# Float64 weights to float32 in five instructions, the scale in one step with the square, the bias as a row on the output, and the output stored by the sync engine

**The chip, the cores and the metric.** One core of a Trainium2 chip. The time is the device time of one execution in microseconds (us), the median over runs. All numbers of profiles are from one profiled execution each, in us from its start, unless ns is said. PE is the tensor engine, PEld its weight loads, DVE the vector engine, ACT the scalar engine, POOL is GpSimd, SP the sync engine; SPq and ACTq are DMA instructions that SP and ACT issue.

## The reference, cut to what matters

```python
kv  = einsum('bhsd,bhse->bhde', k, v)          # (8, 8, 576, 64) each
out = einsum('bhsd,bhde->bhse', q, kv)
x   = out / sqrt(mean(out*out) + 1e-6) * g_norm # to 4608 tokens x 512
r   = maximum(x @ w_in, 0)                      # w_in 512 x 2048, float64
g   = s * (r * r) + b                           # s, b scalars
return g @ w_out                                # w_out 2048 x 512, float64
```

The weights come as float64; the kernel turns them into float32 before it multiplies with them. Since b is one number, `g @ w_out` is `(s r r) @ w_out` plus b times the column sums of w_out, the same row for every token.

## The kernel before

The tokens are worked in twelve tiles T of 384. While the products of tile T run on PE, the attention of tile T+1 is done in 16 steps between them (four pieces of 128 features: turn q, multiply by kv, root mean square, scale). In tile 0 the 32 weight blocks of 128 x 512 are converted at the same time.

```python
    KV_BUFS, AHEAD = 2, 3
    def round_w(i):                      # nine instructions
        nc.vector.tensor_scalar(m <- hi & 0xFFFFF)
        nc.vector.tensor_scalar(e <- (hi >> 20) & 0x7FF)
        nc.scalar.activation(l, lo, AF.Copy, scale=2.0**-52)
        nc.scalar.activation(one_m, m, AF.Copy, bias=1.0, scale=2.0**-20)
        nc.vector.tensor_scalar(e <- clip(e))
        nc.vector.tensor_scalar(e <- (e - 896) * 2**23)
        nc.vector.scalar_tensor_tensor(e <- (hi & sign) | e)
        nc.gpsimd.tensor_tensor(one_m <- one_m + l)
        nc.gpsimd.tensor_tensor(w_sb[i] <- one_m * e)
    ...  # (operands abbreviated)
    def mm1(T, f):
        ...  # four matmuls into h
        nc.scalar.activation(r, h, AF.Relu)
        nc.vector.tensor_mul(r2, r, r)
        nc.vector.tensor_scalar(out=gT[T, f], in0=r2, scalar1=s_col, scalar2=b_col, op0=ALU.mult, op1=ALU.add)
    def mm2(T, j):
        ...  # sixteen matmuls into o
        nc.scalar.copy(o_sb, o)
        nc.scalar.dma_start(out=out_v[...], in_=o_sb)
    ...
    for T in range(NT):
        if 1 <= T and T + 1 < NT:
            load_q(T + 1)                # six DMAs on the sync queue
        ...
        steps = attention(T + 1) if T + 1 < NT else []
        for f in range(FC):              # 16 blocks
            if T == 0:
                w_step(f + 2)            # round_w, then load a weight
            mm1(T, f)
            if steps:
                steps[f]()               # steps[0] turns q of tile T+1 on PE
        if T == 0:
            for i in range(FC + 2, 2 * FC):
                w_step(i)
            ...
        for j in range(J):
            mm2(T, j)
            ...
```

## Time and profile before

| | before |
|---|---|
| time, median of the first 3 runs | 1290.95 us |
| tile 0 ends, tile 1 begins | 264.56 us |
| tiles 1 to 10, up to the start of the last (264.56 to 1203.52) | 938.96 us |
| one plain tile | 92.26 to 92.36 us |
| PE waits after tile 0 | 25.1 us |

The second to fourth rows are starts of the first block of a tile in PE's timeline. A plain tile is one in which no k/v product stands; with one it is 97.5 to 97.8. The profile follows back from the last instruction what released what; this chain says which engine the time hung on (shares of the span):

```profile
PE 68%; DVE 26%; ACT 2%; issue 2%; DMA 1%; SPq 1%; POOLq 0%; DVEq 0%; ACTq 0%
```

A quarter of the span hung on DVE: about 170 us of the chain in tile 0 and about 167 us behind it. The two are not worth the same. Behind tile 0 PE works beside DVE almost all the time and waits for it only 25.1 us, so no more than about that can be won there; a share of the chain is not yet a gain. The other views of before stand in the prediction.

### The profile page before, as it was taken

The numbers are of one execution on the slowest core, as the hardware profiler recorded it, in microseconds if no ns is written. First come the engines' busy times: TensorE is split into PE (matmuls) and PEld (weight loads), VectorE is DVE, ScalarE is ACT, GpSimd is POOL, SyncE is SP. The second block draws the span as 40 slices with busy tenths as digits, with TensorE's granted clock in tenths as the row PEclk, the third lists the DMA queues.
The fourth block names the chain that finished last, engine by engine and source line by source line (L and its number), as shares of the span: only waits on it lengthen the run. The fifth ranks groups of instructions, "written<-read, shape, count | busy, mean of one in ns | idle before, by whom it ended". The sixth has DMA issues, their size and how long they took to land.

```text
span 1289.6 us, 10478 instructions
## 1 busy us (share of the span) xinstructions
PE 1144.8 (89%) x4272; PEld 605.1 (47%) x4272; DVE 499.7 (39%) x700; ACT 206.8 (16%) x397; POOL 89.1 (7%) x72
## 2 busy tenths in 40 slices
PE   3465644899999999999999999999999999999998
PEld 3232411355455455455455454454554554554553
DVE  0499999235035044053053053052153161251220
ACT  0122322021022021021021021020121120120110
POOL 0054456100000000000000000000000000000000
PEclk9998755899999999999999999999999999999999
DMA  9032224300441000000631000001401000000000
GB/s 235 10 93 75 93 98 144 84 9 1 108 114 24 17 9 0 17 9 1 147 74 25 24 1 9 17 0 46 103 1 33 17 1 9 16 1 17 8 1 24
DMA packets 63664, 55.20 MB, mean 43 GB/s; under 512 B 40576, under 2 KB 48768, under 8 KB 63616
## 3 DMA queue, kind: packets, MB, share of 16 engines
q1 hardware_dynamic: 57984, 45.10, 13.6%
q10 hardware_dynamic: 5632, 9.44, 1.9%
q8 instruction: 33, 0.54, 0.2%
q14 instruction: 15, 0.12, 0.0%
HBM read 45.09 MB, written 9.44 MB: 42 GB/s over the span
## 4 chain that ended last, share of the span: by engine, by line
PE 68%; DVE 26%; ACT 2%; issue 2%; DMA 1%; SPq 1%; POOLq 0%; DVEq 0%; ACTq 0%
PE o_ps L294 38%; PE h_ps L277 23%; DVE inv L255 7%; DVE gT L285 4%; PE x_ps L235 3%; DVE r L283 3%; PE ss_ps L249 3%; DVE w_e L141 2%; DVE w_e L138 2%; DVE w_e L132 2%; DVE xT L258 2%; DVE qT L230 1%; PE kv_ps L201 1%; ACT r L281 1%; DVE w_e L144 1%
## 5 line engine op out<-in xcount | busy, mean ns | idle before, releaser
L294 PE MATMUL o_ps<-w,gT 128*128 128x512 f32 x1152 | 517.6, 608 | 40.3 <-POOL w L148 40.3
L277 PE MATMUL h_ps<-xT,w 128*128 128x384 f32 x1536 | 528.7, 493 | 20.1 <-POOL w L148 20.1
L277 PEld LDWEIGHTS h_ps<-xT,w 128*128 128x128 f32 x1536 | 291.0, 193 | 207.9 <-POOL w L148 23.8
L294 PEld LDWEIGHTS o_ps<-w,gT 128*128 128x128 f32 x1152 | 220.8, 194 | 328.2 <-issue 260.6
L283 DVE TENSOR_TENSOR r<-r 128x384 f32<-128x384 f32 x192 | 106.4, 554 | 556.1 <-ACT r L281 556.1
L281 ACT ACTIVATE r<-h_ps 128x384 f32<-128x384 f32 x192 | 93.9, 489 | 377.6 <-PE h_ps L277 363.6
L255 DVE RECIPROCAL inv<-rms 128x384 f32<-128x384 f32 x48 | 122.2, 2545 | 18.5 <-ACT rms L251 18.5
L285 DVE TENSOR_SCALAR gT<-r,s_col,b_col 128x384 f32<-128x384 f32 x192 | 105.3, 548 | 7.9
L235 PE MATMUL x_ps<-qT,bd_kv 128*128 128x192 f32 x192 | 48.1, 378 | 57.8 <-DVE qT L230 57.8
L302 ACT COPY o_sb<-o_ps 128x512 f32<-128x512 f32 x36 | 21.1, 586 | 477.7 <-PE o_ps L294 477.7
L235 PEld LDWEIGHTS x_ps<-qT,bd_kv 128*128 128x128 f32 x192 | 34.3, 209 | 82.9 <-DVE qT L230 79.2
L214 DVE COPY bd_kv<-kv_ps 64x256 f32<-64x256 f32 x8 | 3.4, 422 | 153.9 <-PE kv_ps L201 153.9
L147 POOL TENSOR_TENSOR w_1m<-w_1m,w_l 128x512 f32<-128x512 f32 x32 | 43.2, 1351 | 100.4 <-ACT w_1m L137 100.4
L148 POOL TENSOR_TENSOR w<-w_1m,w_e 128x512 f32<-128x512 f32 x32 | 44.0, 1374 | 43.8 <-DVE w_e L144 42.2
L249 PE MATMUL ss_ps<-sq,ones_bd 128*128 128x384 f32 x96 | 42.2, 523 | 2.4 <-ACT sq L243 2.4
L201 PE MATMUL kv_ps<-v_sb,k_sb 64*64 64x64 f32 x1152 | 25.5, 244 | 19.8 <-DMA v_sb<-in_v_dram 19.8
L137 ACT ACTIVATE w_1m<-w_m 128x512 f32<-128x512 uint32 x32 | 20.2, 630 | 116.2 <-DVE w_m L129 113.1
L201 PEld LDWEIGHTS kv_ps<-v_sb,k_sb 64*64 64x64 f32 x1152 | 22.9, 156 | 27.8 <-issue 23.0
L243 ACT ACTIVATE sq<-x_ps 128x384 f32<-128x384 f32 x48 | 23.5, 490 | 60.5 <-PE x_ps L235 60.5
L258 DVE SCALAR_TENSOR_TENSOR xT<-x_ps,g_col,inv 128x384 f32<-128x384 f32 x48 | 29.6, 617 | 5.3 <-DVE inv L255 0.5
L141 DVE TENSOR_SCALAR w_e<-w_e 128x512 uint32<-128x512 uint32 x32 | 31.1, 973 | 1.1
L251 ACT ACTIVATE rms<-ss_ps,eps_col 128x384 f32<-128x384 f32 x48 | 27.8, 580 | 13.3 <-PE ss_ps L249 13.3
(21 smaller groups left out, 212.1 us busy)
## 6 DMA issues: line engine op xcount, KB each, us to landing
k_sb<-in_k_dram SPq DMA_DIRECT2D x32, 288.0 KB, 4.7
v_sb<-in_v_dram SPq DMA_DIRECT2D x32, 288.0 KB, 5.7
q_sb<-in_q_dram SPq DMA_DIRECT2D x72, 128.0 KB, 3.4
out_dram<-o_sb ACTq DMA_DIRECT2D x36, 256.0 KB, 2.0
w_raw<-in_moe_w_in_dram SPq DMA_DIRECT2D x16, 512.0 KB, 3.8
w_raw<-in_moe_w_out_dram SPq DMA_DIRECT2D x16, 512.0 KB, 3.1
g_col<-in_g_norm_dram ACTq DMA_DIRECT2D x2, 0.2 KB, 2.9
s_col<-in_moe_s_dram ACTq DMA_DIRECT2D x1, 0.5 KB, 5.3
```

Of the source, the lines that this page charges most:

```text
L141: nc.vector.tensor_scalar(out=e, in0=e, scalar1=896.0, scalar2=2.0**23, op0=ALU.subtract, op1=ALU.mult)
L148: nc.gpsimd.tensor_tensor(out=w_sb[i], in0=one_m, in1=e.bitcast(FP32), op=ALU.mult)
L201: nc.tensor.matmul(kv_ps[g][s][l * HB : l * HB + HB, p, :], lhsT=kt[rows, l, j, :], rhs=vt[rows, l, j, :], start=(j == 0), stop=(j == R - 1),)
L235: nc.tensor.matmul(st["x"][:, :, s, :], lhsT=bd[:, s, p, :], rhs=st["qT"][:, :, s, :], start=True, stop=True,)
L249: nc.tensor.matmul(ps, lhsT=ones_bd, rhs=st["sq"], start=True, stop=True)
L255: nc.vector.reciprocal(inv, st["rms"])
L258: nc.vector.scalar_tensor_tensor(xT[T][:, p, :], st["x"].rearrange("p j s t -> p (j s t)"), g_col, inv, ALU.mult, ALU.mult,)
L277: nc.tensor.matmul(h, lhsT=w_in(c, f), rhs=xT[T][:, c, :], start=(c == 0), stop=(c == KC - 1))
L281: nc.scalar.activation(r, h, AF.Relu)
L283: nc.vector.tensor_mul(r2, r, r)
L285: nc.vector.tensor_scalar(out=gT[T, f], in0=r2, scalar1=s_col, scalar2=b_col, op0=ALU.mult, op1=ALU.add)
L294: nc.tensor.matmul(o, lhsT=gT[T, f][:, j * P : j * P + P], rhs=w_out(f), start=(f == 0), stop=(f == FC - 1),)
```

## The change

Its intent: fewer DVE and POOL instructions for a weight, one DVE instruction fewer for each of the 192 blocks of g, and ACT relieved of evicting the output. Cut to its core (one buffer fewer for g, and an earlier load of q for tile 1, are left out):

```diff
-    KV_BUFS, AHEAD = 2, 3
+    KV_BUFS, AHEAD = 3, 4
     def round_w(i):
-        ...  # five DVE, two ACT, two POOL instructions
+            nc.scalar.activation(y, hi, AF.Copy, scale=2.0**-112)
+            nc.scalar.activation(q3, lo, AF.Copy, scale=2.0**-29)
+            nc.vector.tensor_scalar(t <- (y << 3) & 0x7FFFFFFF)
+            nc.vector.scalar_tensor_tensor(t <- (y & sign) | t)
+            nc.gpsimd.tensor_tensor(out=w_sb[i].bitcast(U32), in0=t, in1=q3, op=ALU.add)
+        ...  # for w_out: nc.gpsimd.tensor_tensor adds w_sb[i] to wsum
     def mm1(T, f):
-        nc.vector.tensor_mul(r2, r, r)
-        nc.vector.tensor_scalar(out=gT[T, f], in0=r2, scalar1=s_col, scalar2=b_col, ...)
+        nc.vector.scalar_tensor_tensor(gT[T, f], r, s_col, r, ALU.mult, ALU.mult)
+    def bias_row():
+        nc.tensor.matmul(ps, lhsT=b_sq, rhs=wsum, start=True, stop=True)
+        nc.vector.tensor_copy(out=b_row, in_=ps)
     def mm2(T, j):
-        nc.scalar.copy(o_sb, o)
-        nc.scalar.dma_start(out=out_v[...], in_=o_sb)
+        nc.vector.tensor_tensor(out=o_sb, in0=o, in1=b_row, op=ALU.add)
+        nc.sync.dma_start(out=out_v[...], in_=o_sb)
+    for i in range(AHEAD):
+        load_w(i)                        # now ahead of the fourth k/v load
     for p in range(NP):
         kv_product(0, p)
         ...
+        # three w_steps inside the last quarter of attention(0)
     for T in range(NT):
         ...
         if T == 0:
             for i in range(FC + 3, 2 * FC):
                 w_step(i)
+            bias_row()
```

More of the change, by code (lines that the diff above doesn't have):

```diff
@@ L61 @@
     actp = ctx.enter_context(tc.tile_pool(name="actp", bufs=3))
-    gp = ctx.enter_context(tc.tile_pool(name="gp", bufs=FC + 4))
+    gp = ctx.enter_context(tc.tile_pool(name="gp", bufs=FC + 3))
     outp = ctx.enter_context(tc.tile_pool(name="outp", bufs=3))
@@ L117, in load_w @@
             nc.sync.dma_start(out=dst, in_=src[f * P : f * P + P, :])
+    wsum = const.tile([P, DM], FP32, name="wsum")
     def round_w(i):
-        if not wide:
-            return
-        raw = w_raw.pop(i).rearrange("p (n two) -> p n two", two=2)
-        lo, hi = raw[:, :, 0], raw[:, :, 1]
-        e = rawp.tile([P, DM], U32, name="w_e", tag="w_e", bufs=2)
-        m = rawp.tile([P, DM], U32, name="w_m", tag="w_m", bufs=2)
-        l = rawp.tile([P, DM], FP32, name="w_l", tag="w_l", bufs=2)
@@ L128, in round_w @@
-        one_m = rawp.tile([P, DM], FP32, name="w_1m", tag="w_1m", bufs=2)
-        nc.vector.tensor_scalar(
-            out=m, in0=hi, scalar1=0xFFFFF, scalar2=None, op0=ALU.bitwise_and
-        )
-        nc.vector.tensor_scalar(
-            out=e, in0=hi, scalar1=20, scalar2=0x7FF,
-            op0=ALU.logical_shift_right, op1=ALU.bitwise_and,
-        )
-        nc.scalar.activation(l, lo, AF.Copy, scale=2.0**-52)
-        nc.scalar.activation(one_m, m, AF.Copy, bias=1.0, scale=2.0**-20)
-        nc.vector.tensor_scalar(
-            out=e, in0=e, scalar1=896.0, scalar2=1151.0, op0=ALU.max, op1=ALU.min
-        )
@@ L141, in round_w @@
-        nc.vector.tensor_scalar(
-            out=e, in0=e, scalar1=896.0, scalar2=2.0**23, op0=ALU.subtract, op1=ALU.mult
-        )
-        nc.vector.scalar_tensor_tensor(
-            e, hi, 0x80000000, e, ALU.bitwise_and, ALU.bitwise_or
-        )
-        nc.gpsimd.tensor_tensor(out=one_m, in0=one_m, in1=l, op=ALU.add)
-        nc.gpsimd.tensor_tensor(out=w_sb[i], in0=one_m, in1=e.bitcast(FP32), op=ALU.mult)
+        if wide:
+            raw = w_raw.pop(i)
+            hi = raw.bitcast(FP32).rearrange("p (n two) -> p n two", two=2)[:, :, 1]
+            lo = raw.rearrange("p (n two) -> p n two", two=2)[:, :, 0]
+            y = rawp.tile([P, DM], FP32, name="w_y", tag="w_y", bufs=2)
+            q3 = rawp.tile([P, DM], U32, name="w_q", tag="w_q", bufs=2)
+            t = rawp.tile([P, DM], U32, name="w_t", tag="w_t", bufs=2)
+            nc.scalar.activation(y, hi, AF.Copy, scale=2.0**-112)
+            nc.scalar.activation(q3, lo, AF.Copy, scale=2.0**-29)
+            yb = y.bitcast(U32)
+            nc.vector.tensor_scalar(
+                out=t, in0=yb, scalar1=3, scalar2=0x7FFFFFFF,
+                op0=ALU.logical_shift_left, op1=ALU.bitwise_and,
+            )
+            nc.vector.scalar_tensor_tensor(
+                t, yb, 0x80000000, t, ALU.bitwise_and, ALU.bitwise_or
+            )
+            nc.gpsimd.tensor_tensor(out=w_sb[i].bitcast(U32), in0=t, in1=q3, op=ALU.add)
@@ L150, in w_step @@
+        if i == FC + 1:
+            nc.gpsimd.tensor_tensor(out=wsum, in0=w_sb[FC], in1=w_sb[FC + 1], op=ALU.add)
+        elif i > FC + 1:
+            nc.gpsimd.tensor_tensor(out=wsum, in0=wsum, in1=w_sb[i], op=ALU.add)
     def w_step(i):
@@ L187 @@
     nc.scalar.dma_start(out=b_col, in_=moe_b.to_broadcast((P, 1)))
+    b_sq = const.tile([P, P], FP32, name="b_sq")
+    nc.vector.memset(b_sq, 1.0)
+    nc.vector.tensor_scalar(
+        out=b_sq, in0=b_sq, scalar1=b_col, scalar2=None, op0=ALU.mult
+    )
+    b_row = const.tile([P, DM], FP32, name="b_row")
     kv_ps = {}
@@ L281, in mm1 @@
         nc.scalar.activation(r, h, AF.Relu)
-        r2 = actp.tile([P, N], FP32, name="r2", tag="r2")
-        nc.vector.tensor_mul(r2, r, r)
         gT[T, f] = gp.tile([P, N], FP32, name="gT", tag="g")
-        nc.vector.tensor_scalar(
-            out=gT[T, f], in0=r2, scalar1=s_col, scalar2=b_col, op0=ALU.mult, op1=ALU.add
-        )
+        nc.vector.scalar_tensor_tensor(gT[T, f], r, s_col, r, ALU.mult, ALU.mult)
+    def bias_row():
+        ps = ps_o.tile([P, DM], FP32, name="b_ps", tag="o")
+        nc.tensor.matmul(ps, lhsT=b_sq, rhs=wsum, start=True, stop=True)
+        nc.vector.tensor_copy(out=b_row, in_=ps)
     out_v = out.rearrange("(bp j) n -> bp j n", j=R)
@@ L301, in mm2 @@
         o_sb = outp.tile([P, DM], FP32, name="o_sb", tag="o_sb")
-        nc.scalar.copy(o_sb, o)
+        nc.vector.tensor_tensor(out=o_sb, in0=o, in1=b_row, op=ALU.add)
         g = T // TPG
-        nc.scalar.dma_start(out=out_v[g * P : g * P + P, T % TPG * J + j, :], in_=o_sb)
+        nc.sync.dma_start(out=out_v[g * P : g * P + P, T % TPG * J + j, :], in_=o_sb)
+    for i in range(AHEAD):
+        load_w(i)
     for p in range(NP):
@@ L310 @@
             load_kv(0, p + KV_BUFS)
-    for i in range(AHEAD):
-        load_w(i)
-    for step in attention(0):
+    load_q(1)
+    steps = attention(0)
+    for n, step in enumerate(steps):
         step()
-    load_q(1)
-    for i in range(2):
-        w_step(i)
+        if n >= 12 and n < 15:
+            w_step(n - 12)
     for T in range(NT):
@@ L328 @@
             if T == 0:
-                w_step(f + 2)
+                w_step(f + 3)
             mm1(T, f)
@@ L333 @@
         if T == 0:
-            for i in range(FC + 2, 2 * FC):
+            for i in range(FC + 3, 2 * FC):
                 w_step(i)
+            bias_row()
             for p in range(KV_BUFS):
```

## The prediction

> **What bounds the kernel now.** I read the page's rows of slices first, then the wait table of the tensor engine, then the timelines of four places. The rows (40 slices of 32.2 us) show two programs in one:
>
> ```profile
> PE   3465644899999999999999999999999999999998
> DVE  0499999235035044053053053052153161251220
> POOL 0054456100000000000000000000000000000000
> ```
>
> The reader should see that PE is full from slice 8 on, and that in slices 2 to 6 DVE is full, PE half idle and POOL busy: there the float64 weights are turned into float32 while the first of twelve token tiles runs. The wait table of PE, for the part after tile 0 (264.6 us on), has one entry:
>
> ```profile
> PE x_ps L235 <- DVE qT L230: 25.1, 30, 1.2
> ```
>
> So in 1025 us of steady work PE waits 25.1 us, 30 times some 0.83 us, always for the copy of qT on DVE. Everything else there is PE's own time. In tile 0 the timeline shows why DVE is slow:
>
> ```profile
> 101.74 0.69 DVE L144 SCALAR_TENSOR_TENSOR w_e<-w_raw,w_e 128x512 uint32<-128x512 uint32 x1
> 102.57 1.45 POOL L148 TENSOR_TENSOR w<-w_1m,w_e 128x512 f32<-128x512 f32 x1 [1.15 <-DVE w_e L144]
> 102.93 1.30 DVE L285 TENSOR_SCALAR gT<-r,s_col,b_col 128x384 f32<-128x384 f32 x1
> ...
> 458.27 0.48 DVE L285 TENSOR_SCALAR gT<-r,s_col,b_col 128x384 f32<-128x384 f32 x1
> ```
>
> The same gT instruction takes 1.30 us while POOL runs (it ends 0.2 us after POOL's end at 104.02) and 0.48 us at 458 us, where POOL is silent. The two engines take turns. The stages of tile 0 come from the next lines, again of the timeline:
>
> ```profile
> 70.72 4.73 PE L277 MATMUL h_ps<-xT,w 128*128 128x384 f32 x8 [8.80 <-POOL w L148]
> ...
> 188.37 0.69 DVE L144 SCALAR_TENSOR_TENSOR w_e<-w_raw,w_e 128x512 uint32<-128x512 uint32 x1
> ...
> 192.71 0.69 DVE L144 SCALAR_TENSOR_TENSOR w_e<-w_raw,w_e 128x512 uint32<-128x512 uint32 x1
> ...
> 233.93 30.79 PE L294 MATMUL o_ps<-w,gT 128*128 128x512 f32 x66 [2.20 <-POOL w L148]
> 264.56 2.74 PE L277 MATMUL h_ps<-xT,w 128*128 128x384 f32 x8
> ```
>
> First product from 70.7; one w_out weight each 4.34 us (192.71 minus 188.37) until about 232; one third of the second product is done under that conversion, the last two thirds in 30.8 us; tile 1 starts at 264.56.
>
> [...] 1.30 against 0.48 us above, and L144 (two SBUF inputs) took 1.65 us at 111.55 us, when POOL was at work. [...] Here the square is 0.55 us and the scale 0.48 us, and one operation with two inputs should be near the square's 0.55. [...] behind 6.2 us of waiting (98.5 to 104.75 us) the eight first-product matmuls took 3.98 us, against 2.74 us in the next group.
>
> **The change part by part.**
>
> *a. Start.* Four weight loads (2.1 MB) now stand in the queue ahead of the fourth k/v pair, without which the first attention can't begin. 2048 packets of 1 KB at about 50 ns over 16 DMA engines are 6.4 us. Three conversions move into the last quarter of that attention; most fits into waits of DVE, but the third stands before the reciprocal: about +1.7 us. The wait for the first converted weight after the attention (66 to 70.7) goes, -4.4. First product at 70.7 + 6.4 + 1.7 - 4.4 = 74.4.
>
> *b. First product of tile 0, 16 weights.* Before, four weights took 24.4 us (reciprocals at 95.8 and 120.2), 6.1 each. [...] With turns taken: from the end of the second DVE operation POOL needs 1.59 us (as 102.43 to 104.02), the blocked operation ends 0.2 later, then 0.6 for the next: 2.4 us a weight, four of them 9.7 less the last POOL operation, which hides under the reciprocal, plus copy, reciprocal and scaling of the attention, about 3.6: 12 us. PE needs 12.1 to 13 us for the same four (270.9 to 283.9 in tile 1 is 13.0, with a 0.83 wait in it). I take 13 for the coupling of the two, times four, plus 2 for the cold clock: 54 us. It ends near 129.
>
> *c. Conversion of the last 13 weights.* ACT 1.3 us a weight, DVE 1.1, POOL two operations (the addition and the running column sum), together about 2.7 us as the contiguous pair of before. DVE's first operation slips in between them, the second costs its 0.55 and a 0.15 handover: 3.45 us, 45 us in all, plus 1 for two sums under b. It ends near 175. (Before: 4.34.)
>
> *d. The bias row.* Its matmul stands ahead of the whole second product and needs all weights, so no third of it is hidden any more: 2 cold matmuls 1.8 us, then 96 x 0.449 = 43.1, and 1.2 for the clock (30.79 before, against 66 x 0.449 = 29.6). Tile 1 begins at 175 + 46 = 221, against 264.6: -43.6; rounded -43.
>
> *e. gT in one operation.* DVE loses 0.45 to 0.5 us per block; two blocks stand in front of each of the late qT copies (gT before the reciprocal and after it), so the copy comes 0.9 us earlier and the 0.83 us wait goes: up to -25, I take -24.
>
> *f. The output moves to DVE and the sync queue.* Eviction 0.75 us by DVE instead of 0.59 by ACT, hidden. But sync issues in program order. Before, it held loads alone and fetched q a tile ahead. Now the load of q for tile T+1 stands behind the three stores of tile T-1, the last of which waits for the end of that tile; and PE wants this q right after the first block of tile T. The listing of the changed kernel's instructions confirms it: three stores, then six q loads, for T = 1 to 10. Sizes, from the timeline and the q tile's own view:
>
> ```profile
> 403.24 3.99 SPq L92 DMA_DIRECT2D q_sb<-in_q_dram  x6
> ...
> DMA to landing us min/median/max: 2.7/3.1/3.3
> ...
> 454.57 0.59 ACT L302 COPY o_sb<-o_ps 128x512 f32<-128x512 f32 x1 [13.15 <-PE o_ps L294]
> ...
> 455.19 0.34 ACTq L304 DMA_DIRECT2D out_dram<-o_sb  x1
> 456.63 0.14 PEld L228 LDWEIGHTS qT_ps<-ident,q_sb 128*128 128x128 f32 x1
> 456.95 0.49 PE L228 MATMUL qT_ps<-ident,q_sb 128*128 128x128 f32 x3
> ```
>
> From the end of the product (454.5): eviction to 455.3, store issued by 455.8, sixth q load issued five steps of 0.665 later at 459.1, landed 3.2 later at 462.3; PE wants it at 457.2. Stall 5.1 us, in seven tiles; in the three tiles that follow a k/v product (2.5 us of other work for PE) 2.6 us: 43.5. The clock after 5 us of idling: about +1.5 each, 0.3 after the short ones: 11.4. Together +55.
>
> Sum: 1291 - 43 - 24 + 55 = 1279 us.
>
> **The rivals.** R1: the q loads arrive in time, since q is double-buffered, and nothing is given back: 1291 - 67 = 1224. For it: q has two buffers and DMA has room. Against: the order on one queue; a buffer does not help a load that has not been issued. R2: the stalls are worse, each with a full return to the cold clock (2.1 us measured after 6.2 us of idling), the stores delaying q in the DMA engines, and no gain in e because DVE is behind after each stall: 1291 - 43 + 75 = 1323. Against: after the stall all four blocks of DVE work lie behind PE as before. R3: POOL is still the bound of tile 0, the integer addition slower than the float one (1.27 to 1.31 us unhindered)[...]: +7 to +12, 1286 to 1291. The trace has DVE getting in between two contiguous POOL operations[...].
>
> **Range and chances.** Tile 0 I trust to 9 us, e to 5, f to 12; together about 16: 1262 to 1298 for 8 in 10. Faster by 2% is under 1265, which needs a stall near 4 us or a tile 0 ten us better: 0.16. Slower by 2% is over 1317, near R2: 0.05. Within 2%: 0.79.
>
> **What would show it.** In the profile of the changed kernel: tile 1 begins near 221; POOL has 47 additions of 128x512 (32 conversions, 15 sums), and a w_out weight takes about 3.45 us; PE is idle from about 130 to 175; the wait table after tile 0 has nothing left of x_ps for qT and instead ten waits of qT_ps for a q load, up to 5 us each, and tiles 3 to 4 us longer than before (1025 us over eleven tiles, 93 each). If PE's wait for q is absent, f is wrong and R1 holds; if POOL's addition is longer than 1.4 us without a DVE operation beside it, c is wrong; if tiles after a stall show matmuls at double length for more than 3 us, R2 holds.

The sum stays 1291 - 43 - 24 + 55 = 1279 us. What stands behind its steps, from the trace and the page of before:

- *Turns of DVE and POOL* (steps b and c): L285 takes 1.30 us beside POOL and 0.48 without, L144 1.65 (at 111.55) and 0.69 (at 101.74). How the two engines come to exclude each other is not shown. The sentence cut in b counted, for a weight, three DVE operations (two of the conversion, and gT) and one of POOL.
- *DVE between two POOL operations* (c): POOL's operations at 184.86 and 186.15 us follow without a gap; DVE's L132, begun at 184.97, ends at 186.47, 0.3 us after the first of them, and L138 then begins under the second.
- *Clock*: behind 6.2 us of waiting, four x_ps matmuls took 1.65 us (at 104.75; 0.81 at 270.05) and eight of the first product 3.98 (at 106.19; 2.74 at 110.66), at a granted clock of 0.50 from 104.75 to 108.0: 2.1 us more in all. The 2 us in b and the 1.5 and 0.3 in f are estimates; beside them stand the first block of tile 0, 4.73 us against 2.74, and the block at 95.68, 2.85 us behind a wait of 2.05. Two 128 x 512 matmuls at a granted clock of 0.50 took 2.07 us (186.23), where d takes 1.8.
- *50 ns a packet* (a): the page has 57984 packets of q1 in 13.6% of 16 engines' 1289.6 us, 48 ns each on the mean.
- *R3* had a second case; the range of +7 to +12 stood for both.

## The result, and the profile after

| | before | after |
|---|---|---|
| time, median | 1290.99 us (4 runs) | 1281.97 us (4 runs, 1281.34 to 1285.44) |
| tile 1 begins | 264.56 | 219.89 |
| from there to the start of the last tile | 938.96 | 974.08 |
| plain tiles | 92.26 to 92.36 | 92.38 to 98.09 |

The ratio is 0.9934, with a 95% interval of 0.992 to 0.9948: within 2%. A ratio is the mean time of one kernel's fast runs over that of the other's in the same rounds, so it isn't quite the ratio of the medians.

So tile 0 won 44.7 us and the other tiles gave 35.1 back. The same rows of slices of the changed kernel, with the granted clock of PE as a fourth:

```profile
PE   2488059999999899899999899899999899899998
DVE  0378930330340240240241241241241141141110
POOL 0033840000000000000000000000000000000000
PEclk9999569999999899999899899999999999999999
```

The conversion ends two slices earlier (POOL has nothing from slice 6 on, counted from 0; before from slice 8), but PE, which before was half busy under it, is empty in slice 4. And behind it there are slices of 8 in the rows of PE and of its clock, which before had none there. The chain of the changed kernel names the new holder:

```profile
PE 84%; DMA 4%; SPq 4%; DVE 4%; issue 2%; POOL 2%; ACT 1%; POOLq 0%; DVEq 0%; ACTq 0%
```

DVE fell from 26% to 4% (from about 170 to 38 us in tile 0, from 167 to 8 behind it). DMA and SPq, 2% together before, are 8%. The wait table of PE from 235 us on shows which DMA:

```profile
PE qT_ps L236 <- DMA q_sb<-in_q_dram: 35.2, 23, 4.1
```

The 25.1 us of x_ps for qT are gone, and in their place stand 35.2 us of the transposes of q for the load of q; two more waits, 4.3 us, lie in the first stall, just before 235: 39.5 us in all. One of the ten stalls, at the start of tile 3, in the order of time (start, length, then the engine):

```profile
415.54 2.74 PE L285 MATMUL h_ps<-xT,w 128*128 128x384 f32 x8
415.74 0.69 DVE L312 TENSOR_TENSOR o_sb<-o_ps,b_row 128x512 f32<-128x512 f32 x1 [13.04 <-PE o_ps L304]
416.46 0.33 SPq L314 DMA_DIRECT2D out_dram<-o_sb  x1
416.84 4.02 SPq L92 DMA_DIRECT2D q_sb<-in_q_dram  x6
422.42 0.89 PE L236 MATMUL qT_ps<-ident,q_sb 128*128 128x128 f32 x2 [4.13 <-DMA q_sb<-in_q_dram]
424.31 0.47 PE L236 MATMUL qT_ps<-ident,q_sb 128*128 128x128 f32 x1 [1.01 <-DMA q_sb<-in_q_dram]
424.58 5.16 PE L285 MATMUL h_ps<-xT,w 128*128 128x384 f32 x8
```

PE begins tile 3 at 415.54. Only then can DVE evict the last output of tile 2, SP store it, and SP send, from 416.84 on, for the q that PE wants as soon as its first block is done, near 418.2. PE stands for 4.13 us, then for 1.01, and the next block of eight matmuls takes 5.16 us instead of 2.75. Tile 0, from the timeline:

```profile
143.36 1.60 POOL L150 TENSOR_TENSOR wsum<-wsum,w 128x512 f32<-128x512 f32 x1
144.92 1.44 POOL L146 TENSOR_TENSOR w<-w_t,w_q 128x512 uint32<-128x512 uint32 x1
...
175.27 2.07 PE L296 MATMUL b_ps<-wsum,b_sq 128*128 128x512 f32 x2 [45.57 <-POOL wsum L150]
177.14 42.92 PE L304 MATMUL o_ps<-w,gT 128*128 128x512 f32 x96
219.89 2.74 PE L285 MATMUL h_ps<-xT,w 128*128 128x384 f32 x8
```

POOL has two operations a weight without a gap, 3.08 us a weight (the sum before this one began at 140.28). PE waits 45.6 us for the last of them, then does the bias row and the whole second product of tile 0.

### The profile page after: what moved, and what is told of

Its sections match the earlier page's. It is cut to its first block, busy times and chain, and to the rows that moved or that the text cites. A ratio compares the mean times of both kernels' runs of the same rounds, so it can differ in the third digit from the quotient of the medians.

```text
span 1280.2 us, 10164 instructions
## 1 busy us (share of the span) xinstructions
PE 1141.2 (89%) x4274; PEld 608.5 (48%) x4274; DVE 382.3 (30%) x451; ACT 187.4 (15%) x361; POOL 69.8 (5%) x55
## 4 chain that ended last, share of the span: by engine, by line
PE 84%; DMA 4%; SPq 4%; DVE 4%; issue 2%; POOL 2%; ACT 1%; POOLq 0%; DVEq 0%; ACTq 0%
PE o_ps L304 39%; PE h_ps L285 37%; PE x_ps L243 3%; SPq L92 3%; PE ss_ps L257 3%; DMA q_sb<-in_q_dram 3%; DVE inv L263 2%; POOL w L146 1%; PE qT_ps L236 1%; DMA k_sb<-in_k_dram 1%; DMA v_sb<-in_v_dram 1%; PE kv_ps L209 1%; DVE o_sb L312 1%; POOL wsum L150 0%; DVE gT L291 0%
## 5 line engine op out<-in xcount | busy, mean ns | idle before, releaser
L285 PE MATMUL h_ps<-xT,w 128*128 128x384 f32 x1536 | 539.0, 501 | 2.7 <-DVE xT L266 2.7
L304 PE MATMUL o_ps<-w,gT 128*128 128x512 f32 x1152 | 499.5, 594 | 0.0
L285 PEld LDWEIGHTS h_ps<-xT,w 128*128 128x128 f32 x1536 | 297.1, 197 | 193.8 <-issue 21.3
L291 DVE SCALAR_TENSOR_TENSOR gT<-r,s_col 128x384 f32<-128x384 f32 x192 | 120.7, 629 | 338.6 <-ACT r L289 338.6
L312 DVE TENSOR_TENSOR o_sb<-o_ps,b_row 128x512 f32<-128x512 f32 x36 | 24.9, 691 | 442.7 <-PE o_ps L304 442.7
L236 PE MATMUL qT_ps<-ident,q_sb 128*128 128x128 f32 x144 | 31.6, 310 | 40.8 <-DMA q_sb<-in_q_dram 39.5
L236 PEld LDWEIGHTS qT_ps<-ident,q_sb 128*128 128x128 f32 x144 | 20.8, 153 | 64.1 <-issue 50.7
L146 POOL TENSOR_TENSOR w<-w_t,w_q 128x512 uint32<-128x512 uint32 x32 | 44.7, 1397 | 103.6 <-DVE w_t L143 94.0
L296 PE MATMUL b_ps<-wsum,b_sq 128*128 128x512 f32 x2 | 2.1, 1140 | 45.6 <-POOL wsum L150 45.6
L238 DVE COPY qT<-qT_ps 128x384 f32<-128x384 f32 x48 | 26.5, 551 | 40.5 <-PE qT_ps L236 40.5
L143 DVE SCALAR_TENSOR_TENSOR w_t<-w_y,w_t 128x512 uint32<-128x512 uint32 x32 | 34.4, 1075 | 1.1
L139 DVE TENSOR_SCALAR w_t<-w_y 128x512 uint32<-128x512 uint32 x32 | 30.9, 965 | 6.0 <-ACT w_y L136 6.0
L259 ACT ACTIVATE rms<-ss_ps,eps_col 128x384 f32<-128x384 f32 x48 | 27.8, 580 | 12.7 <-PE ss_ps L257 12.7
```

Of the source, the lines that this page charges most:

```text
L146: nc.gpsimd.tensor_tensor(out=w_sb[i].bitcast(U32), in0=t, in1=q3, op=ALU.add)
L236: nc.tensor.transpose(ps[:, j, :], q_in[T][:, j, 2 * p : 2 * p + 2, :], ident)
L285: nc.tensor.matmul(h, lhsT=w_in(c, f), rhs=xT[T][:, c, :], start=(c == 0), stop=(c == KC - 1))
L291: nc.vector.scalar_tensor_tensor(gT[T, f], r, s_col, r, ALU.mult, ALU.mult)
L304: nc.tensor.matmul(o, lhsT=gT[T, f][:, j * P : j * P + P], rhs=w_out(f), start=(f == 0), stop=(f == FC - 1),)
L312: nc.vector.tensor_tensor(out=o_sb, in0=o, in1=b_row, op=ALU.add)
```

## The experiments

**Theory.** Three things make up the result: a shorter tile 0; the qT wait that went with the shorter gT; and the q load, which stands on one queue behind the stores of the tile before, so that PE waits and then works at half clock for a while (granted 0.50 for 3.41 or 6.83 us at a time, experiment 4). **Rivals** are named with each run: the eviction on DVE, the traffic of stores beside loads, a wait that only moves. All ten runs ended with a correct result within the comparison's tolerance; their time is the median of four executions, and the kernel before took 1291.6 to 1291.9 us beside them. The changed kernel was not run again beside them; its 1281.97 us is from its own rounds. Three parts of the change were never taken alone: the third k/v buffer, the fourth weight in flight, and the three conversions inside the first attention.

**Experiment 1: the stores issued by ACT again.** The changed kernel with

```diff
-        nc.sync.dma_start(out=out_v[...], in_=o_sb)
+        nc.scalar.dma_start(out=out_v[...], in_=o_sb)
```

> The changed kernel with its output stores issued by ScalarE again; all else as changed. Theory (issue order: a q load stands behind the stores and comes 4 us late, and PE then works at half clock for a while): the ten waits of qT_ps for q (39.5 us) and the slower matmuls after them (about 21 us, worked out as 1060 us for the tiles 1 to 11 minus 1025 before, plus 25 of x_ps waits gone, minus 39.5) all go: 1282 - 60 = 1222 us, within 6. Rival (the rest of the change costs the time: eviction on DVE, a later gT, or DMA traffic of stores beside loads whoever issues them): little or nothing is won, 1270 to 1282 us.

Measured: 1219.76 us, ratio 0.9441 (0.9427 to 0.9455). The wait table of PE from 215 us on is empty, every plain tile takes 89.5 to 89.7 us, and the time from the start of tile 1 to that of the last is 911.33 us, 62.75 less than the 974.08 of the changed kernel. The rival falls: eviction on DVE and the late gT, which stayed, cost nothing that can be seen.

**Experiment 2: stores on the sync queue, q ahead of them.** The changed kernel with

```diff
-        if 1 <= T and T + 1 < NT:
-            load_q(T + 1)
...
+        if T + 2 < NT:
+            load_q(T + 2)
         for j in range(J):
             mm2(T, j)
```

> The changed kernel with its stores still on the sync queue, but the q load of tile T+2 issued ahead of the three stores of tile T instead of after them. Theory (only the order on the one queue matters): as good as giving the stores back to ScalarE, 1222 us within 6, no wait of PE for q. Rival (one queue for loads and stores is too little: the stores delay the loads in the engines, or sync has no time to issue both): PE still waits for q or k/v, 1245 us or more.

Measured: 1218.54 us, ratio 0.9435 (0.9421 to 0.9449), no different from experiment 1, and no wait of PE for q. So neither the number of queues nor the traffic matters here, only what stands in front of the q load in the order of issue.

**Experiment 3: the kernel before with the stores on the sync queue,** nothing else:

```diff
-        nc.scalar.dma_start(out=out_v[...], in_=o_sb)
+        nc.sync.dma_start(out=out_v[...], in_=o_sb)
```

> The kernel before with nothing changed but the stores, issued by the sync engine. Theory: it pays the ten waits (39.5 us) and the half clock after them (about 21 us), while its own x_ps waits stay as they are: 1291 + 60 = 1351 us, within 10. Rival (in the changed kernel the waits came from its lighter DVE or its other buffers, not from the store): 1291 to 1300 us.

Measured: 1353.9 us, ratio 1.0482 (1.0467 to 1.0498). PE's waits after tile 0:

```profile
PE qT_ps L228 <- DMA q_sb<-in_q_dram: 39.8, 24, 4.2
PE x_ps L235 <- DVE qT L230: 25.2, 30, 1.2
```

One word in one line costs 62 us; the q wait comes on top of the old x_ps wait and leaves it as it was.

**Experiment 4: PE kept at work during the stall.** The changed kernel with

```diff
             mm1(T, f)
+            if f == 0 and T in (1, 3, 4, 6, 7, 9, 10):
+                d_ps = ps_o.tile([P, DM], FP32, name="d_ps", tag="o")
+                for n in range(4):
+                    nc.tensor.matmul(d_ps, lhsT=w_in(0, 0), rhs=w_out(0), start=(n == 0), stop=(n == 3))
             if steps:
```

> The changed kernel with four extra 128x512 matmuls (about 3.6 us, their result unused) between the first block and the first transposes in the seven tiles where PE waits about 4.5 us for q, so that PE is not idle there. Theory (the part of the loss above the waits themselves is the clock that drops while PE idles): waits shrink to below 1 us in these tiles at no cost, and the slower matmuls after them go: 7 tiles x about 2.1 us = 15 us less, 1267 us within 5. Rival (the loss is something else, such as DVE and ACT being filled again after the wait): no gain, 1282 us, or a loss by the extra work.

Measured: 1272.51 us (1270.34 to 1274.77), ratio 0.9846 (0.9829 to 0.9862): 9.5 us less than the changed kernel, not 15. Tile 3 again:

```profile
418.95 3.60 PE L345 MATMUL d_ps<-w,w 128*128 128x512 f32 x8
422.93 0.30 PE L236 MATMUL qT_ps<-ident,q_sb 128*128 128x128 f32 x1 [0.39 <-PE d_ps L345]
423.49 0.33 PE L236 MATMUL qT_ps<-ident,q_sb 128*128 128x128 f32 x1 [0.25 <-DMA q_sb<-in_q_dram]
424.63 0.33 PE L236 MATMUL qT_ps<-ident,q_sb 128*128 128x128 f32 x1 [0.82 <-DMA q_sb<-in_q_dram]
424.80 2.75 PE L285 MATMUL h_ps<-xT,w 128*128 128x384 f32 x8
```

The transposes begin 6.6 us after the tile does, against 6.9 in the changed kernel, so hardly earlier, but the block behind them takes 2.75 us instead of 5.16. In all seven tiles it is 2.75, against 3.87 to 5.16 in the changed kernel. Work without any use makes the kernel faster, because PE's clock stays up (mean granted clock 0.975, against 0.962): for this part the rival (DVE and ACT filled again after the stall) falls. The seven tiles gained 11.4 us together (691.35 to 679.91 us), 1.6 each. The other 2 us went in the three tiles without the extra work (94.74, 95.13 and 94.93 us against 94.25, 96.10 and 92.38): behind their stalls, 2.8 to 3.2 us here and 2.2 to 3.0 there, the block took 4.44 us in all three here, and 4.27, 5.33 and 2.75 in the changed kernel. The profile's granted clock says more. Behind its ten stalls the changed kernel has nine stretches at clock 0.50, of 3.41 us (six of them) or 6.83 us (tiles 3, 5 and 6), and none in tile 8; their starts (228.05, 327.03, 422.61 us and so on to 1105.27) lie whole multiples of 3.41 us apart in this trace. The length of the stall alone does not decide: behind the 3.0 us of tile 5 the clock was 0.50 for 6.83 us, behind the 4.2 us of tile 7 for 3.41. What else decides is not shown. PE is busy for 35.8 us in these stretches, so about 18 us went to the clock in all (an estimate: half of that time). The expectation was too large because part of the 2.1 us a tile is not clock; that the rest is the transposes, which wait for their q loads one by one, is argued and not shown. In the profiled run, the slowest of the four, tile 1 also began 1.8 us later than in the changed kernel, so its span is only 7.6 us shorter.

**Experiment 5: gT in one operation, alone.** The kernel before with the gT of the changed kernel and no b at all (wrong; the comparison passed all the same):

```diff
-        nc.vector.tensor_mul(r2, r, r)
-        nc.vector.tensor_scalar(out=gT[T, f], in0=r2, scalar1=s_col, scalar2=b_col, ...)
+        nc.vector.scalar_tensor_tensor(gT[T, f], r, s_col, r, ALU.mult, ALU.mult)
```

> The kernel before with gT in one operation (s goes in with the square) and b left out, so the result is wrong on purpose; conversion, eviction, stores as before. Theory: after tile 0 the 30 waits of PE for the qT copy go (25 us), and in tile 0 each of 16 blocks loses about 1.2 us of DVE (0.55 + 1.30 become about 0.6): 1291 - 25 - 19 = 1247 us, within 6. Rival (the wait moves to another operation of DVE, or DVE in tile 0 only waits longer for POOL): 1275 to 1291 us.

Measured: 1254.69 us, ratio 0.9713 (0.9698 to 0.9727). After tile 0 it is the theory: no x_ps wait is left, a plain tile takes 89.55 us instead of 92.26, and ten tiles (255.33 to 1166.76) gain 27.5 us. In tile 0 the rival is half right: tile 1 begins 9.2 us earlier, not 19. The timeline of DVE says why:

```profile
104.83 0.61 DVE L283 SCALAR_TENSOR_TENSOR gT<-r,s_col 128x384 f32<-128x384 f32 x1
105.36 1.49 DVE L129 TENSOR_SCALAR w_m<-w_raw 128x512 uint32<-128x512 uint32 x1
```

gT takes 0.61 us now (the square alone took 0.55), and the next operation, which took 0.41 before, takes 1.49 us. Taking away the instruction that was long beside POOL (1.30 us) made the next one long here. That it waits for POOL is inferred from this length: in experiment 10, where POOL has nothing in this phase, the shift in the same place takes 0.42.

**Experiment 6: the new conversion, alone.** The kernel before with the five instructions of the changed kernel in `round_w`, no column sum, gT and bias as before.

> The kernel before with the new conversion alone (five instructions, no sum of the weights, gT and bias as before). Theory: in the first product of tile 0 a weight falls from 6.1 to about 3.8 us (16 x 2.3 = 37), each of the last 14 from 4.34 to about 2.4 us (27), and the first third of the second product stays hidden: 1291 - 62 = 1229 us, within 10; that is more than the 44.7 us that tile 0 won in the changed kernel, where the column sum and the bias row take some back. Rival (the conversion is bound elsewhere, by ACT or by the loads): tile 0 wins no more than 45 us, 1246 us or more.

Measured: 1224.62 us, ratio 0.9485 (0.9471 to 0.9499). Tile 1 begins at 200.69, 63.9 us earlier than before, where the changed kernel won 44.7. The sum is right, its parts less so: a late weight takes 2.02 us (expected 2.4), a weight of the first product about 4.3 (expected 3.8; four of them lie between 112.51 and 129.71 us in PE's timeline, in which PE waits 3.29 us for qT).

**Experiment 7: the bias matmul behind the first third of the second product,** stores on ACT:

```diff
-            bias_row()                   # ahead of mm2(0, 0)
     def mm2(T, j):
         ...                              # the sixteen matmuls
+        if T == 0 and j == 0:
+            bias_row()
```

> The changed kernel with stores on ScalarE, and the bias matmul moved from ahead of the second product of tile 0 to behind its first third, so that this third can run under the conversion of the last weights. Theory: 1222 - 12 = 1210 us within 5 (14 of 16 weights x 0.9 us hidden). Rival (PE at half clock in that phase hinders nothing but also gains nothing, as the third then starts cold twice): 1218 to 1222 us.

Measured: 1207.57 us (one of four 1203.7), ratio 0.9341 (0.9327 to 0.9356): 12.2 us less than experiment 1. The third that lay open in the changed kernel is hidden again. (The profiled run is the one of 1203.7 us; in it tile 1 begins 16.6 us earlier than in experiment 1, so the profile shows some 4 us more than the median.)

**Experiment 8: the bias row summed by PE.** As experiment 7, without the column sum on POOL:

```diff
             nc.tensor.matmul(o, lhsT=gT[T, f][...], rhs=w_out(f), ...)
+            if b_ps is not None:         # T == 0 and j == 0
+                nc.tensor.matmul(b_ps, lhsT=b_sq, rhs=w_out(f), start=(f == 0), stop=(f == FC - 1))
```

> The changed kernel with stores on ScalarE, no running column sum on POOL; the bias row is summed by PE instead, one extra matmul a weight beside the first third of the second product. Theory: POOL has one operation a weight instead of two, so the last weights go from 3.08 to about 2.4 us each (13 x 0.7 = 9 us) on top of the 12 us of the hidden third: 1222 - 21 = 1201 us within 6. Rival (PE with two products a weight becomes the bound of that phase): 1208 us or more.

Measured: 1191.96 us, ratio 0.9227 (0.9211 to 0.9242), 27.8 less than experiment 1. POOL's additions:

```profile
138.38 1.31 POOL L145 TENSOR_TENSOR w<-w_t,w_q 128x512 uint32<-128x512 uint32 x1 [0.69 <-DVE w_t L142]
140.40 1.32 POOL L145 TENSOR_TENSOR w<-w_t,w_q 128x512 uint32<-128x512 uint32 x1 [0.70 <-DVE w_t L142]
```

A late weight takes 2.02 us instead of 3.08: POOL's 1.32, then 0.70 in which it waits for DVE's operation with two inputs (begun 0.22 us after POOL's, it takes 1.64 us beside it; 0.69 at 135.53, when POOL was idle). The expectation (2.4) had put the shift on the path too; it starts 0.22 us before POOL's operation (138.16 and 138.38 us) and runs off the path. The time is 9 us under the expectation, more than its 6 us allow, and these 0.38 us a weight make about 5 (an estimate, for 13 weights). What makes the rest is not separated. One thing that differs is PE's clock: the mean granted clock of the profiled run is 0.997 here, with the extra matmuls, and 0.979 in experiment 1.

**Experiment 9: the first weight loads behind the fourth k/v load,** on experiment 8:

```diff
-    for i in range(AHEAD):
-        load_w(i)
     for p in range(NP):
         kv_product(0, p)
         ...
+    for i in range(AHEAD):
+        load_w(i)
     load_q(1)
```

> The kernel with the bias row summed on PE, the stores on ScalarE, and the first four weight loads moved back behind the fourth k/v load, where the kernel before had them. Theory (step a of the prediction: these 2.1 MB in front of the k/v pair delay the first attention by about 6.4 us, and the weights are not needed before 61 us): tile 1 begins 6 us earlier, 1192 - 6 = 1186 us within 2. Rival (the first conversions then wait for their weights, or the DMA engines had room anyway): 1190 to 1192 us.

Measured: 1184.46 us, ratio 0.9169 (0.9153 to 0.9184), 7.5 us less than experiment 8. The last k/v product of the first group, in the changed kernel and here:

```profile
35.23 2.19 PE L209 MATMUL kv_ps<-v_sb,k_sb 64*64 64x64 f32 x70 [0.66 <-DMA v_sb<-in_v_dram]
```

```profile
28.54 2.19 PE L204 MATMUL kv_ps<-v_sb,k_sb 64*64 64x64 f32 x70 [1.09 <-DMA v_sb<-in_v_dram]
```

It comes 6.7 us earlier, and tile 1 as well (192.57 to 185.82). This is the fastest version, 8% below the kernel before.

**Experiment 10: the integer addition on DVE instead of POOL,** on experiment 1:

```diff
-            nc.gpsimd.tensor_tensor(out=w_sb[i].bitcast(U32), in0=t, in1=q3, op=ALU.add)
+            nc.vector.tensor_tensor(out=w_sb[i].bitcast(U32), in0=t, in1=q3, op=ALU.add)
```

> The changed kernel with stores on ScalarE (1220 us) and the integer addition of the conversion moved from POOL to DVE[...], so that POOL has nothing in the first product of tile 0 and only the running sum after it. Theory[...]: in the first product gT takes 0.61 and the shift 0.42 us each time and four weights take about 12.5 instead of 13.7 us; in the last 13 weights the sum (1.3) and three DVE operations (about 1.65) still add up to about 3.0 us instead of 3.08; in all 1215 us within 4. Rival (the two engines do not exclude each other, DVE operations are just longer in that phase for another reason such as the loads): a late weight takes about 1.7 us, 13 x 1.4 = 18 us less, about 1200 us.

Measured: 1216.12 us, ratio 0.9418 (0.9404 to 0.9432), in the range expected, but not by the terms expected. In the late weights POOL now has one operation of 1.32 us (at 144.80 in its timeline), DVE three:

```profile
144.57 0.42 DVE L139 TENSOR_SCALAR w_t<-w_y 128x512 uint32<-128x512 uint32 x1
145.02 1.64 DVE L143 SCALAR_TENSOR_TENSOR w_t<-w_y,w_t 128x512 uint32<-128x512 uint32 x1
146.80 0.69 DVE L146 CUSTOM_DVE_ANT_0 w<-w_t,w_q 128x1024 uint16<-128x1024 uint16 x1
147.41 0.42 DVE L139 TENSOR_SCALAR w_t<-w_y 128x512 uint32<-128x512 uint32 x1
```

A weight takes 2.84 us, near the 3.0 of turns and far from the 1.7 of engines that don't exclude each other: the operation with two inputs takes 1.64 us under POOL's sum and 0.69 alone. The other half of the expectation failed. In the first product gT and the shift do take 0.61 and 0.42 us each time, yet four weights take as long as ever (from the reciprocal at 88.51 to that at 102.54, 14.0 us; 14.1 in the changed kernel, 88.11 to 102.21). The reason is on DVE: in these two stretches it is busy for 12.7 us here and 12.9 there. The four additions that it took over cost 0.69 us each, 2.8 in all, and that is what its waits for POOL had cost: in the changed kernel three shifts take 0.81 to 1.44 us there and one gT 1.53, 2.9 us more than 0.42 and 0.61. So the run exchanges one for the other, and whether the turns set the first product it cannot say. DVE also has gaps there in which it waits for ACT's first step of the conversion (0.56 and 0.68 us in this run). (The trace lists the addition as CUSTOM_DVE_ANT_0 on 128x1024 uint16, 0.69 us.)

## Why the prediction was right

By its steps, with the measured size:

| step | predicted | measured | from |
|---|---|---|---|
| a. first product can go on (its first six matmuls ran from 68.72) | 74.4 | 74.64 | timeline after |
| b. first product ends | near 129 | 129.7 | timeline after |
| c. a late weight | 3.45 us | 3.08 us | POOL's timeline |
| c. conversion ends | near 175 | 175.27 | bias matmul |
| d. tile 1 begins | 221 | 219.89 | PE's timeline |
| tile 0 in all | -43 | -44.7 | 264.56 to 219.89 |
| e. shorter gT | -24 | -27.6 | 938.96 to 911.33, experiment 1 |
| f. waits for q | +43.5 | +39.5 | wait tables |
| f. clock and the rest | +11.4 | +23.2 | 62.75 - 39.5 |
| sum | -12 | -9.4 | spans 1289.6 to 1280.2 |

**Tile 0** came out within 2 us, and experiments 6 to 9 show that its main steps were the right ones: the weights ahead of k/v cost 6.7 us, against the 6.4 worked out (experiment 9), and the uncovered third 12.2, against the 12.6 that 14 x 0.9 gives (experiment 7). In b, 13 us were taken for four weights and 14.1 measured; how much of it the turns of DVE and POOL make was argued, and experiment 10 does not show it. The end of c, 175, was right by luck: c was too long by 0.37 us a weight, 4.8 in all, while DVE reached the late weights 5 us after b ended, because the last reciprocal stood before them (the second operation of the first late one starts at 134.97 us); the two errors cancel.

The sum is in part luck too: the clock cost 11.8 us more than was taken, while tile 0 (1.7), the shorter gT (3.6) and the waits for q (4.0) came out 9.3 us better, so that it is only some 3 us off.

**e** was right in kind and size; experiment 5 has it alone (27.5). It is 2.7 us a tile: three waits of 0.83 and 0.2 us beside them.

**f** was the step that decided between R1 and the rest. The wait came out at 4.2 to 5.1 us in the long stalls against 5.1 predicted (the eviction took 0.69 us, against 0.75). The term that was mis-sized is the clock: +1.5 us for a long stall and +0.3 for a short one were taken, and the tiles show 2.1 to 3.4 for the seven long ones (17.0 together) and 2.3, 3.5 and 0.6 for the short ones. Experiment 4 shows that most of it, 1.6 us a long stall, is the clock. Short stalls were taken to cost 0.3 us; behind two of three the granted clock was 0.50, and the block took 4.27 and 5.33 us instead of 2.75.

**R1** (the loads arrive in time) is what experiments 1 and 2 made true: 1219.76 and 1218.54, where R1 said 1224. **R2** (1323) took the clock nearly right (2.1 us a stall, against 2.3 on the mean) and the rest wrong. Its sign, matmuls at double length for more than 3 us, did show: half clock lasted 3.41 or 6.83 us behind nine of the ten stalls. **R3** did not occur: POOL's integer addition takes 1.27 us unhindered.

The change as a whole is so small because its two good parts (experiments 5 and 6, 37 and 67 us each on its own; they overlap in tile 0) share it with three placements that nobody needed: stores before q (62.8 us), the bias matmul before the product (12.2), weights before k/v (6.7), and with a column sum on POOL, one of the two busiest engines there (DVE 41.3 and POOL 41.8 of the 45.6 us from 129.7 to 175.3). With those four undone it is 107 us faster than before instead of 9.

## What to carry to other kernels

When a store moves to the queue that issues the loads, ask for each load behind it when it is wanted: here the store was issued at the end of its tile, the q loads behind it inherited that time in spite of two buffers, and it cost 62.75 us (experiment 1; 62 in experiment 3). A small difference between two kernels may be the sum of large ones with opposite signs; take the parts singly before calling a change neutral. Where a trace shows an operation longer while another engine works (0.69 us alone and 1.64 beside POOL, experiment 10), count the operations of both engines together; here, removing the one that was long (1.30 us) made the next one long (1.49, experiment 5).
